# A table for PSUM tiles, an earlier ELU remainder and earlier cluster assignments in a fused attention and feed-forward kernel

## The chip, the cores and the metric

The kernel runs on one core of one Trainium2 chip. The metric is the device time of one execution in microseconds (us), as a median of several runs. The engines of the core are named as the profile names them: PE (TensorE, the matmuls; PEld its weight loads), DVE (VectorE), ACT (ScalarE), POOL (GpSimd) and SP (SyncE, which issues the DMAs here). Each engine works through its own queue of instructions in the order in which the program issues them, and waits for others by semaphores.

## The reference

```python
def _attn_ref(q, k, v, centroids):          # 4 batches, 8 heads, 768 tokens, 64 wide; 16 centroids a head
    q_assign = np.argmax(np.einsum('bhsd,hcd->bhsc', q_n, c_n), axis=-1)   # rows normalized
    k_assign = np.argmax(np.einsum('bhsd,hcd->bhsc', k_n, c_n), axis=-1)
    mask = q_assign[:, :, :, None] == k_assign[:, :, None, :]
    scores = np.where(mask, scale * np.matmul(q, k.transpose(0, 1, 3, 2)), -1000000000.0)
    attn = softmax(scores)
    return np.matmul(attn, v)

def _moe_ref(x, w_in, w_out):               # x: 3072 x 512, w_in: 512 x 2048, w_out: 2048 x 512
    h = x @ w_in
    g = np.where(h > 0.0, h, np.exp(np.minimum(h, 0.0)) - 1.0)
    return g @ w_out
```

The attention output, brought to 3072 tokens of 512, is the x of the second part. A query attends only to the keys that were assigned to the same centroid.

## The kernel before, in words

Work is cut into 48 blocks: 4 batches, each of 3 thirds of the queries (256 of them), each of 4 pairs of heads. One loop (lines 780 to 858) goes over the block number n and issues all instructions in an order that is written out by hand (the pool's scheduler is switched off in line 89). In one pass it issues, in this order: the values of the block before, `values(n - 1)`; what is left in a list, `finish()`; loads; the scores of block n, `scores(n)`; transposes for the next batch in passes 8 to 11 of a batch; and then two to four steps of the feed-forward part (`main`), which runs LAG = 7 blocks behind. `extra` hangs further steps behind single steps of `main`. So a pass is marked by what `main` holds, which repeats every four passes, `(n - 7) % 4`. The change calls it the kind:

- kind 0: two hidden products, `hidden` 0 and 1 (called h0 and h1 below)
- kind 1: two hidden products, `hidden` 2 and 3, and a `finish()` behind them
- kind 2: four of the seven products with w_out (`outer`, lines 651 to 717)
- kind 3: the other three

A batch has 12 blocks. Its last (n = 11, 23, 35) is of kind 0, the first of the next batch of kind 1.

The pieces that the steps below touch:

- `scores` (482 to 545): three units u0, u1, u2 of 128 x 2 x 512 each. A unit's matmuls (line 490) fill one pair of PSUM banks, ACT takes the exponential of it into p (line 513). In the first batch a further matmul per half adds a mask (line 502); in the others `keep_same` (442 to 456) zeroes on DVE, after the exponential, what belongs to other clusters, twelve instructions of line 449 per block. It needs kc and qc, the cluster numbers of keys and queries, which small matmuls (lines 417 and 430) and ACT copies (420 and 438) prepare.
- `sums` (547 to 551): three DVE additions that shrink the six parts of p for the row sums.
- `values` (553 to 598): o_bank takes p times v (line 572), a tile d takes the row sums (line 561). ACT reads d twice (590, 591), copies o_bank (592) and takes an exponential (593); DVE (594, 595) and POOL (598) finish the reciprocal and the scaling.
- `hidden` (606 to 626): 32 matmul instructions (line 613) into one pair tile, an exponential on ACT (623), a clamp on POOL (624). The remainder, `elu` (628 to 639), reads the pair tile once more on DVE (line 630) and then forms a difference (632 or 634). It isn't issued at once: `hidden` puts it into the list `lag`, and the next `finish()` issues it, which is that of the next `hidden`, or the one behind `values` in the next pass.
- `similar` (362 to 376): products of queries (j = 0) or keys (j = 1) with the centroids, for half of the tokens (line 369), and a DVE transpose out of PSUM (376). `assign` (378 to 405): reduce, compare, transpose on DVE (388, 392, 402), which gives the cluster rows `hot`. For the next batch both products are issued in the last pass of a batch, the assignment of the queries there too, that of the keys in the first pass of the next batch (lines 786 to 788).

PSUM has three pair tiles and two single banks, o_bank and f_bank. The pair tiles come from a pool with three buffers: every call of `banks()` gets a new tile, and the pool gives it a buffer that has been released by its last reader in the order of the program. In steady passes, with the buffers called A, B and C, this gives, as the program built from the kernel before has it:

| kind | d | u0, u1, u2 | hidden |
|---|---|---|---|
| 0 | C | B, A, C | B, A |
| 1 | C | B, C, B | A, C |
| 2 | B | A, C, B | |
| 3 | A | C, B, A | |

Of the kernel before, what the change touches and what calls it, by code (L numbers as in the profile page):

```python
# [9 lines left out]
F32 = mybir.dt.float32  # L10
# [7 lines left out]
PSUM = bass.MemoryType.PSUM  # L18

P = 128  # L20
# [41 lines left out]
def main_path(ctx, tc, c, q, k, v, centroids, moe_w_in, moe_w_out, out):  # L62
# [21 lines left out]
    probs = ctx.enter_context(tc.tile_pool(name="probs", bufs=NT // 2))  # L84
    work = ctx.enter_context(tc.tile_pool(name="work", bufs=2))
    xtp = ctx.enter_context(tc.tile_pool(name="xtp", bufs=2))
    short = ctx.enter_context(tc.tile_pool(name="short", bufs=3, space=PSUM))
    long = ctx.enter_context(tc.tile_pool(name="long", bufs=1, space=PSUM))
    ctx.enter_context(tc.manual_schedule())

# [1 line left out]
    o_bank = long.tile([P, 512], F32, name="o_bank")  # L92
    f_bank = long.tile([P, 512], F32, name="f_bank")

    def banks():
        return short.tile([P, 2, 512], F32, name="banks", tag="banks")


    g = const.tile([P, FC, QS], F32, name="gT")
# [259 lines left out]
                else:  # L359
                    nc.vector.tensor_copy(to[:, :, m], of)  # L360

    def similar(b, j, at, size):

        if at == 0:
            sim[b, j] = route.tile([P, S], F32, name="sim", tag="sim", bufs=1)
        ps = banks()[:, 0]
        cols = slice(at, at + size)
        for pr in range(NPR):
            nc.tensor.matmul(
                ps[32 * pr : 32 * pr + 32, :size],  # L370
                lhsT=cT[:, 32 * pr : 32 * pr + 32],
                rhs=T[b * NPR + pr, j][:, cols],
                start=True,
                stop=True,
            )
        return lambda: nc.vector.transpose(sim[b, j][:, cols], ps[:, :size])  # L376
# [34 lines left out]

    def key_numbers(b):

        ps = banks()[:, 0]
        kc[b] = route.tile([P, NT, H], F32, name="kc", tag="kc", bufs=2)
        for kt in range(NT):
            nc.tensor.matmul(
                ps[:, ts(kt, H)], lhsT=hot[b, 1][:, 0, ts(kt, P)], rhs=index, start=True, stop=True
            )
        nc.scalar.copy(kc[b].rearrange("p t h -> p (t h)"), ps[:, : NT * H])  # L420
# [21 lines left out]
    def keep_same(n):  # L442

        b, third, pr = blocks[n]
        for u in range(NT // 2):
            for e in range(2):
                for m in range(2):
                    p = pu[n, u][:, e, ts(m, QS)]
                    nc.vector.scalar_tensor_tensor(  # L449
                        p,  # L450
                        qc[b, third][:, 2 * pr + e],
                        kc[b][:, 2 * u + m, 2 * pr + e : 2 * pr + e + 1],
                        p,
                        op0=Alu.is_equal,
                        op1=Alu.mult,
                    )
# [18 lines left out]
    LAG = 7  # L475
# [2 lines left out]

    blocks = [(b, third, pr) for b in range(B) for third in range(NQ) for pr in range(NPR)]
    pu, osum, xT = {}, {}, {}  # L480

    def scores(n):
        b, third, pr = blocks[n]
        i = b * NPR + pr
        cols = ts(third, QS)

        def plain(s, kt):
            for e in range(2):
                rows = slice(64 * e, 64 * e + 64)
                nc.tensor.matmul(  # L490
                    s[:, e, ts(kt % 2, QS)],
                    lhsT=T[i, 1][rows, ts(kt, P)],
                    rhs=T[i, 0][rows, cols],
                    start=n > 0 or kt % 2 == 0,
                    stop=b > 0,
                    skip_group_check=n == 0,
                )

        def mask(s, kt):
            for e in range(2):  # L500
                rows = slice(64 * e, 64 * e + 64)
                nc.tensor.matmul(
                    s[:, e, ts(kt % 2, QS)],
                    lhsT=hot[b, 1][rows, side(pr, e), ts(kt, P)],
                    rhs=qm[n][rows],
                    start=False,
                    stop=True,
                    skip_group_check=n == 0,
                )

        def exponentials(s, u):
            p = pu[n, u] = probs.tile([P, 2, 2 * QS], F32, name="p", tag="p")
            nc.scalar.activation(p, s, Act.Exp, scale=SCALE)  # L513

        if n == 0:

            turn_first = similar(0, 1, 0, QS)
            turn_rest = similar(0, 1, QS, 2 * QS)
            units = [banks() for _ in range(2)]
            for u in range(2):  # L520
                for m in range(2):
                    plain(units[u], 2 * u + m)
            turn_first()
            for u in range(NT // 2):
                assign(0, 1, u * QS, QS)
                if u == 0:
                    turn_rest()
                if u == 1:
                    units.append(banks())
                    for m in range(2):  # L530
                        plain(units[2], 4 + m)
                for m in range(2):
                    mask(units[u], 2 * u + m)
                exponentials(units[u], u)
                weigh(1)
            return
        for u in range(NT // 2):
            s = banks()
            for m in range(2):
                plain(s, 2 * u + m)  # L540
                if b == 0:
                    mask(s, 2 * u + m)
            exponentials(s, u)
            if n < LAG + 3:
                weigh(1)
# [7 lines left out]
    def values(n):  # L553

        b, third, pr = blocks[n]
        d = banks()[:, 0]
        summed = osum.pop(n, None)

        def row_sums(p, m, kt, last):
# [46 lines left out]
        lag.clear()  # L606

    def hidden(b, third, n):
        h = banks()
        hf = h.rearrange("p a (f s) -> p (a f) s", f=2)  # L610
        for ch in range(KC):
            for f in range(4):
                nc.tensor.matmul(  # L613
                    hf[:, f],
                    lhsT=w_in[:, ch, ts(4 * n + f, P)],
                    rhs=xT[b, third][:, ch],
                    start=(ch == 0 and f % 2 == 0),
                    stop=(ch == KC - 1),
                    skip_group_check=True,
                )  # L620
        t = g[:, 4 * n : 4 * n + 4]

        nc.scalar.activation(t, hf, Act.Exp)  # L623
        nc.gpsimd.tensor_scalar(t, t, 1.0, 0.0, op0=Alu.min, op1=Alu.max)  # L624
        finish()
        lag.append(lambda: elu(n, t, hf))
# [103 lines left out]
    turns = {8: 0, 9: 1, 10: 2, 11: 3}  # L730
    groups = [g for b in range(B) for third in range(NQ) for g in mlp(b, third)]

    def clusters(b, j):
        for half in range(2):
            similar(b, j, half * HS, HS)()

    def load_v(n):
        b, third, pr = blocks[n]
# [21 lines left out]

    def verdict():
        ok = c["ok"]
        ps = banks()[:, 0]
        nc.tensor.matmul(ps[:1, :1], lhsT=ok[:, 3:4], rhs=ones[:, :1], start=True, stop=True)
        nc.vector.tensor_copy(c["go"], ps[:1, :1])

# [10 lines left out]
        assign(0, 0, half * HS, HS)  # L777
    masks(0)

    for n in range(len(blocks) + LAG):  # L780
        b, at = n // NB, n % NB
        ahead = b + 1 < B
        if n <= len(blocks) and n > 0:
            values(n - 1)
        finish()
        if at == 0 and 0 < b < B:
            for half in range(2):
                assign(b, 1, half * HS, HS)
        if ahead:
            for pr in {5: [0], 6: [1], 9: [2], 10: [3]}.get(at, []):  # L790
                load("q", (b + 1) * NPR + pr)
# [19 lines left out]
        if n < len(blocks):  # L811
            late = [lambda n=n: sums(n)] if n >= LAG + 3 else []
            if b > 0:
                third = at // NPR
                q_in = lambda b, third, places: (lambda: query_numbers(b, third, places))
                if at == 0:
                    extra[0] = [
                        lambda b=b: key_numbers(b),
                        q_in(b, third, [(0, f_bank), (1, o_bank)]),
                        lambda n=n: keep_same(n),  # L820
                    ] + late
                    extra[1] = [
                        lambda b=b, third=third: query_numbers(
                            b, third, [(2, f_bank), (3, banks()[:, 0])]
                        )
                    ]
                else:
                    if at % NPR == 0:
                        query_numbers(b, third, [(0, f_bank), (1, o_bank)])
                        extra[0] = [q_in(b, third, [(2, f_bank), (3, o_bank)])]  # L830
                    keep_same(n)
                    if len(main) == 3 and at % NPR == 2:
                        extra[1] = late
                    else:
                        late and late[0]()
            else:
                late and late[0]()
        if ahead and at + 1 == NB:

            extra[0] = [lambda b=b: clusters(b + 1, 0)]  # L840
            extra[1] = [
                lambda b=b: [assign(b + 1, 0, half * HS, HS) for half in range(2)],
                lambda b=b: clusters(b + 1, 1),
            ]
        for m, step in enumerate(main):
            step()
# [266 lines left out]
```

## Time and profile before

| what | us |
|---|---|
| median of 3 runs | 1018.0 (1017.7 to 1018.22) |
| the profiled execution, its own time | 1019.75 |
| its span, first to last instruction | 1017.6 |
| PE busy | 989.8 |
| DVE busy | 658.3 |
| ACT busy | 324.0 |
| POOL busy | 136.3 |
| mean granted PE clock | 0.994 of full speed |

The profile is one execution, recorded instruction by instruction. Its times are us from the start of the span. A row of the timeline has the start, the busy time, the engine, the line of the kernel, what is written from what and how many instructions were put together; in brackets stands how long the engine had been idle before and what ended that. A row of the waits has the waiting engine with its tile and line, what it waited for, and then the total, the number and the longest of these waits. Matmuls are pipelined and their ends are modelled, so that a busy PE isn't always a PE at its peak.

### The profile page before, as it was taken

How to read it: one execution, taken by the hardware profiler on the slowest of the kernel's cores; microseconds unless marked ns; L12 is line 12 of the kernel's file. 1: busy time of each engine (PE TensorE's matmuls, PEld its weight loads, DVE VectorE, ACT ScalarE, POOL GpSimd, SP SyncE). 2: the span in 40 equal slices, each digit the busy share in tenths (PEclk: the TensorE clock that was granted, in tenths of full speed). 3: DMA queues.
4: the chain of work that ended last, by engine and by line, in shares of the span. 5: the costliest groups of instructions: out<-in, count | busy, mean ns of one | idle time of the engine just before them, and what ended most of it. 6: DMA issues, size and time to landing. Idle time of an engine off the chain costs nothing.

```text
span 1017.6 us, 14770 instructions
## 1 busy us (share of the span) xinstructions
PE 989.8 (97%) x5989; PEld 773.3 (76%) x5989; DVE 658.3 (65%) x1182; ACT 324.0 (32%) x576; POOL 136.3 (13%) x145
## 2 busy tenths in 40 slices
PE   6999999999999999999999999999999999999997
PEld 4566777778878878777778778767887887888886
DVE  7999972576666667849567568577765665673121
ACT  6777422341242233222323232214223323321010
POOL 0010130110210210210111111111021021021010
PEclk9999999999999999999999999999999999999999
DMA  9857122000132122100122113101010010000000
GB/s 291 310 167 195 48 52 59 26 23 16 37 67 43 37 49 61 37 17 17 52 47 47 53 28 67 43 10 32 16 38 19 29 37 16 32 21 1 21 0 24
DMA packets 103963, 55.59 MB, mean 55 GB/s; under 512 B 83408, under 2 KB 96720, under 8 KB 103888
## 3 DMA queue, kind: packets, MB, share of 16 engines
q1 hardware_dynamic: 103888, 54.57, 19.3%
q8 instruction: 49, 0.80, 0.3%
q14 instruction: 26, 0.21, 0.1%
HBM read 48.27 MB, written 6.29 MB: 54 GB/s over the span
## 4 chain that ended last, share of the span: by engine, by line
PE 74%; DVE 17%; ACT 4%; issue 3%; DMA 1%; POOL 0%; DVEq 0%; ACTq 0%; POOLq 0%
PE banks L613 27%; PE f_bank L643 15%; PE o_bank L643 11%; PE o_bank L572 10%; PE banks L490 8%; DVE p L449 3%; DVE ex L265 2%; PE banks L561 2%; ACT p L513 1%; DVE w_in L268 1%; DVE w_out L268 1%; DVE w_in L271 1%; DVE ex L287 1%; DVE psum L550 1%; DVE w_out L271 1%
## 5 line engine op out<-in xcount | busy, mean ns | idle before, releaser
L613 PE MATMUL banks<-xT,w_in 128*128 128x256 f32 x1536 | 344.2, 384 | 4.3 <-DVE sim L376 3.9
L613 PEld LDWEIGHTS banks<-xT,w_in 128*128 128x128 f32 x1536 | 291.3, 191 | 54.1 <-DVE sim L376 6.1
L449 DVE SCALAR_TENSOR_TENSOR p<-qc,kc,p 128x256 f32<-128x256 uint8 x432 | 184.8, 500 | 18.2 <-ACT qc L438 18.1
L490 PE MATMUL banks<-qT,kT 64*128 64x256 f32 x1152 | 147.8, 389 | 5.6 <-ACT p L513 4.5
L572 PE MATMUL o_bank<-p,v_raw 128*64 128x256 f32 x1152 | 144.7, 386 | 2.4 <-DMA v_raw<-in_v_dram 1.6
L623 ACT ACTIVATE gT<-banks 128x1024 f32<-128x1024 f32 x48 | 49.1, 1024 | 293.4 <-PE banks L613 293.4
L513 ACT ACTIVATE p<-banks 128x1024 f32<-128x1024 f32 x144 | 140.2, 1033 | 4.0 <-PE banks L490 2.9
L490 PEld LDWEIGHTS banks<-qT,kT 64*128 64x128 f32 x1152 | 101.1, 186 | 45.1 <-PE o_bank L572 10.0
L572 PEld LDWEIGHTS o_bank<-p,v_raw 128*64 128x64 f32 x1152 | 78.2, 137 | 55.9 <-issue 14.5
L594 DVE TENSOR_TENSOR e<-e,r 128x256 f32<-128x256 f32 x48 | 20.4, 424 | 144.3 <-ACT r L593 144.3
L630 DVE SCALAR_TENSOR_TENSOR gT<-gT,banks 128x1024 f32<-128x1024 f32 x48 | 58.3, 1215 | 78.1 <-POOL gT L624 78.0
L624 POOL TENSOR_SCALAR gT<-gT 128x1024 f32<-128x1024 f32 x48 | 54.1, 1127 | 350.4 <-ACT gT L623 324.5
L590 ACT ACTIVATE r<-banks 128x256 f32<-128x256 f32 x48 | 18.4, 383 | 243.4 <-PE banks L561 243.4
L643 PE MATMUL o_bank<-w_out,gT 128*128 128x256 f32 x416 | 95.1, 382 | 0.0
L598 POOL TENSOR_TENSOR xT<-xT,r 128x256 f32<-128x256 f32 x48 | 40.2, 837 | 409.0 <-DVE r L595 354.4
L643 PEld LDWEIGHTS o_bank<-w_out,gT 128*128 128x128 f32 x416 | 78.2, 190 | 13.5 <-ACT p L513 2.0
L643 PE MATMUL f_bank<-w_out,gT 128*128 128x256 f32 x352 | 79.6, 379 | 0.0
L643 PEld LDWEIGHTS f_bank<-w_out,gT 128*128 128x128 f32 x352 | 66.9, 190 | 9.1
L643 PE MATMUL f_bank<-w_sum,gT 128*128 128x256 f32 x224 | 50.9, 380 | 0.5 <-DVE o_sb L683 0.2
L550 DVE TENSOR_TENSOR psum<-psum,p 128x1024 f32<-128x1024 f32 x38 | 50.2, 1322 | 1.4
L643 PEld LDWEIGHTS f_bank<-w_sum,gT 128*128 128x128 f32 x224 | 42.3, 190 | 7.4 <-DVE o_sb L683 1.7
L549 DVE TENSOR_TENSOR psum<-p 128x1024 f32<-128x1024 f32 x38 | 46.1, 1214 | 0.0
(130 smaller groups left out, 835.2 us busy)
## 6 DMA issues: line engine op xcount, KB each, us to landing
v_raw<-in_v_dram SPq DMA_DIRECT2D x48, 384.0 KB, 3.1
w_sum<-in_moe_w_out_dram SPq DMA_DIRECT2D x12, 512.0 KB, 5.3
out_dram<-o_sb SPq DMA_DIRECT2D x24, 256.0 KB, 2.0
q_raw<-in_q_dram SPq DMA_DIRECT2D x48, 96.0 KB, 3.3
k_raw<-in_k_dram SPq DMA_DIRECT2D x48, 96.0 KB, 2.9
w_sum<-in_moe_w_in_dram SPq DMA_DIRECT2D x8, 512.0 KB, 9.8
w_out<-in_moe_w_in_dram SPq DMA_DIRECT2D x8, 512.0 KB, 10.9
w_out<-in_moe_w_out_dram SPq DMA_DIRECT2D x4, 512.0 KB, 3.4
```

Source lines behind the costliest of these rows:

```text
L449: nc.vector.scalar_tensor_tensor(p, qc[b, third][:, 2 * pr + e], kc[b][:, 2 * u + m, 2 * pr + e : 2 * pr + e + 1], p, op0=Alu.is_equal, op ...
L490: nc.tensor.matmul(s[:, e, ts(kt % 2, QS)], lhsT=T[i, 1][rows, ts(kt, P)], rhs=T[i, 0][rows, cols], start=n > 0 or kt % 2 == 0, stop=b > 0 ...
L513: nc.scalar.activation(p, s, Act.Exp, scale=SCALE)
L549: nc.vector.tensor_tensor(to, pu[n, 0], pu[n, 1], op=Alu.add)
L550: nc.vector.tensor_tensor(to, to, pu[n, 2], op=Alu.add)
L572: nc.tensor.matmul(o_bank[64 * e : 64 * e + 64, :QS], lhsT=raw["v", n][:, e, kt], rhs=p[:, e, ts(m, QS)], start=(kt == 0), stop=(kt == NT ...
L598: nc.gpsimd.tensor_tensor(x, x, r, op=Alu.mult)
L613: nc.tensor.matmul(hf[:, f], lhsT=w_in[:, ch, ts(4 * n + f, P)], rhs=xT[b, third][:, ch], start=(ch == 0 and f % 2 == 0), stop=(ch == KC - 1),
L623: nc.scalar.activation(t, hf, Act.Exp)
L624: nc.gpsimd.tensor_scalar(t, t, 1.0, 0.0, op0=Alu.min, op1=Alu.max)
L630: nc.vector.scalar_tensor_tensor(t, t, -1.0, hf, op0=Alu.add, op1=Alu.max)
L643: nc.tensor.matmul(to[:, :QS], lhsT=left[:, f], rhs=right[:, f], start=(f == 0), stop=(f == FC // 2 - 1),)
```

## The change

The pool's three rotating buffers become three fixed pair tiles. `banks(i)` returns tile i modulo 3; without an argument (the start of the kernel) it takes turns. In the loop a table `place` says for each kind of block which tile d, the three units and the two hidden products use, counted from `at_tile`, which moves on by one in the passes of kinds 2 and 3 and in the first passes. In kind 1, u2 has the tile of h1; in kind 2, d and u1 share one.

For n > LAG, `finish()` is called in front of `values(n - 1)` too, so that a remainder left over from the pass before is issued ahead of the values.

In the last block of a batch both halves of one centroid product go to the two halves of one pair tile: the queries to u2's, the keys to h0's. The sums of that block move behind the query products, and the key assignment moves from the first pass of the next batch to the end of this one. In the first block of a batch the key numbers go to f_bank, and they, the numbers of the first head pair and `keep_same` are issued ahead of the hidden products; the numbers of the other pairs follow in two groups instead of one. At the very start the key products of block 0 go to o_bank and f_bank.

```diff
-    short = ctx.enter_context(tc.tile_pool(name="short", bufs=3, space=PSUM))
+    short = ctx.enter_context(tc.tile_pool(name="short", bufs=1, space=PSUM))
...
-    def banks():
-        return short.tile([P, 2, 512], F32, name="banks", tag="banks")
+    pair_tiles = [short.tile([P, 2, 512], F32, name=f"banks{n}") for n in range(3)]
+    turn_of = 0
+
+    def banks(i=None):
+        nonlocal turn_of
+        if i is None:
+            i = turn_of
+            turn_of = (turn_of + 1) % 3
+        return pair_tiles[i % 3]
...
-    def similar(b, j, at, size):
+    def similar(b, j, at, size, ps=None):
...
-        ps = banks()[:, 0]
+        if ps is None:
+            ps = banks()[:, 0]
...
     def key_numbers(b):
-        ps = banks()[:, 0]
+        ps = f_bank
...
-            turn_first = similar(0, 1, 0, QS)
-            turn_rest = similar(0, 1, QS, 2 * QS)
+            turn_first = similar(0, 1, 0, QS, o_bank)
+            turn_rest = similar(0, 1, QS, 2 * QS, f_bank)
...
         for u in range(NT // 2):
-            s = banks()
+            s = banks(place["u"][u])
...
-        d = banks()[:, 0]
+        d = banks(place["d"])[:, 0]
...
-        h = banks()
+        h = banks(place["h"][n % 2])
...
-    def clusters(b, j):
+    def clusters(b, j, i):
+        ps = banks(i)
+        for turn_half in [similar(b, j, half * HS, HS, ps[:, half]) for half in range(2)]:
+            turn_half()
+
+    def tell(b, j):
         for half in range(2):
-            similar(b, j, half * HS, HS)()
+            assign(b, j, half * HS, HS)
...
+    at_tile = turn_of
     for n in range(len(blocks) + LAG):
...
+        kind = (n - LAG) % 4 if n >= LAG else None
+        if kind == 1:
+            place.update(d=at_tile, u=[at_tile + 1, at_tile, at_tile + 2], h=[at_tile + 1, at_tile])
+        elif kind == 2:
+            place.update(d=at_tile + 2, u=[at_tile + 1, at_tile + 2, at_tile])
+        else:
+            place.update(d=at_tile, u=[at_tile + 1, at_tile + 2, at_tile])
+            place.update(h=[at_tile + 1, at_tile + 2])
+        if kind not in (0, 1):
+            at_tile += 1
+        if n > LAG:
+            finish()
         if n <= len(blocks) and n > 0:
             values(n - 1)
         finish()
-        if at == 0 and 0 < b < B:
-            for half in range(2):
-                assign(b, 1, half * HS, HS)
...
                 if at == 0:
-                    extra[0] = [
-                        lambda b=b: key_numbers(b),
-                        q_in(b, third, [(0, f_bank), (1, o_bank)]),
-                        lambda n=n: keep_same(n),
-                    ] + late
-                    extra[1] = [
-                        lambda b=b, third=third: query_numbers(
-                            b, third, [(2, f_bank), (3, banks()[:, 0])]
-                        )
-                    ]
-                else:
...
+                    key_numbers(b)
+                    query_numbers(b, third, [(0, o_bank)])
+                    extra[0] = [q_in(b, third, [(1, f_bank), (2, o_bank)])]
+                    extra[1] = [q_in(b, third, [(3, f_bank)])]
+                elif at % NPR == 0:
+                    query_numbers(b, third, [(0, f_bank), (1, o_bank)])
+                    extra[0] = [q_in(b, third, [(2, f_bank), (3, o_bank)])]
+                keep_same(n)
+            if b > 0 and at % NPR == 2:
+                extra[1] = late
+            elif not ahead or at + 1 < NB:
                 late and late[0]()
         if ahead and at + 1 == NB:
-            extra[0] = [lambda b=b: clusters(b + 1, 0)]
+            extra[0] = [lambda b=b, i=place["u"][2]: clusters(b + 1, 0, i)] + late
             extra[1] = [
-                lambda b=b: [assign(b + 1, 0, half * HS, HS) for half in range(2)],
-                lambda b=b: clusters(b + 1, 1),
+                lambda b=b: tell(b + 1, 0),
+                lambda b=b, i=place["h"][0]: clusters(b + 1, 1, i),
+                lambda b=b: tell(b + 1, 1),
             ]
```

## The prediction

> **What bounds the kernel.** I read the page's busy times first, then the waits of TensorE (PE), then the timeline around each wait, and last the stretches with the granted clock.
>
> ```profile
> PE 989.8 (97%) x5989; PEld 773.3 (76%) x5989; DVE 658.3 (65%) x1182; ACT 324.0 (32%) x576; POOL 136.3 (13%) x145
> ```
>
> PE is busy 989.8 of 1017.6 us, so the change can win only what PE loses. Of its waits (total us, times, longest) four fall on what the diff touches:
>
> ```profile
> PE banks L490 <- ACT p L513: 4.5, 10, 1.2
> PE banks L613 <- DVE sim L376: 3.9, 2, 2.0
> ...
> PE banks L490 <- DVE gT L630: 1.2, 3, 0.4
> ...
> PE banks L561 <- DVE psum L551: 0.5, 3, 0.2
> ```
>
> They understate the loss, since a matmul counts as busy until its modelled end (some 0.38 us, while the next starts 0.22 later). So I take the distance of starts in the timeline. Undisturbed, a block's 24 score matmuls take 2.79 us (start 261.05, next work 263.84), a hidden group of 32 takes 7.00 to 7.11, a pair of centroid products (x16) 1.43, a block's values 2.64 + 0.53.
>
> First place: kind 1, the block after a third's first two hidden groups.
>
> ```profile
> 281.02 2.11 PE L490 MATMUL banks<-qT,kT 64*128 64x256 f32 x16
> ...
> 282.40 1.95 ACT L513 ACTIVATE p<-banks 128x1024 f32<-128x1024 f32 x2
> ...
> 283.37 1.22 DVE L630 SCALAR_TENSOR_TENSOR gT<-gT,banks 128x1024 f32<-128x1024 f32 x1
> 283.49 1.14 PE L490 MATMUL banks<-qT,kT 64*128 64x256 f32 x8 [0.36 <-ACT p L513]
> ```
>
> The third unit stands still until the first unit's exponential is over (about 283.4): both got one pair tile, since h1, the hidden product just made, is still held by its remainder (L630), queued on DVE behind the values' L594/L595. Next work starts at 284.56: 3.54 us instead of 2.79. Natural start of the third unit: 282.93.
>
> Second place: the last block of a batch.
>
> ```profile
> 427.40 1.50 PE L369 MATMUL banks<-qT,cT 128*32 128x384 f32 x16
> ...
> 428.62 1.16 POOL L624 TENSOR_SCALAR gT<-gT 128x1024 f32<-128x1024 f32 x1 [7.74 <-ACT gT L623]
> 428.91 1.41 DVE L551 TENSOR_TENSOR psum<-psum 128x512 f32<-128x512 f32 x1
> 430.24 1.03 DVE L376 STREAM_TRANSPOSE sim<-banks 128x384 f32<-128x384 f32 x2
> 430.86 8.86 PE L613 MATMUL banks<-xT,w_in 128*128 128x256 f32 x32 [1.97 <-DVE sim L376]
> ```
>
> The second hidden group wants a tile that a transpose (L376) must empty, which stands behind the sums (L549 to L551). And the 8.86 us show a second price. Columns: busy us (count) of PE, PEld, DVE, ACT, POOL, then clock, DMA share, GB/s:
>
> ```profile
> 427.40:431.00 3.60, 1.63 (x18) 0.55 (x18) 3.53 (x5) 1.03 (x1) 1.16 (x1) 1.00 0.00 0
> 431.00:434.00 3.00, 3.00 (x10) 2.51 (x11) 2.93 (x5) 0.00 (x0) 0.00 (x0) 0.67 0.00 0
> ```
>
> After 1.97 us of idleness the granted clock fell to 0.67 in the next 3 us.
>
> **What the old order loses, by batch end.** At the second and third (427, 670): 2.04 (3.47 for the products instead of 1.43) + 1.78 (8.79 for the group instead of 7.01) + 0.83 (scores at 444.25: 3.62) + 0.99 after it (values at 462.86: 2.99 instead of 2.64, row sums 1.04 instead of 0.53, scores 2.92: DVE reached mask and sums late, since the key and query numbers came behind a hidden group) = 5.64. The first (188) has 0.16 + 0.83 + 0.99 = 1.98; there no masking on DVE delays the sums.
>
> **The change, part by part.**
> - *Table, kind 1.* u2 takes h1's tile, and finish() moves in front of the values, so L630 is queued ahead of L594. In the case shown the clamp (L624) of h1 ends at 280.10 and DVE is idle from 275.2 to 282.56: L630 runs 280.1 to 281.3, L632 to 282.0, both before u2's 282.93 and before L594's 282.56. The 0.75 goes, but for 0.05 (u1 waits for the reader of d as before). Six such blocks: 6 x 0.70 = 4.2. If the idle DVE stretch were gone, this would be 0. The seventh (115.3, first batch) waits 1.3; there L630 follows weight work that ends at 114.8, so it ends at 116.0 instead of letting PE go at 116.81: 0.75.
> - *Table, kind 2.* d now sits in u1's tile, not u2's. Kind 1 shows what that costs: u1 started 0.98 after u0 instead of 0.93. About nine blocks x 0.05 = -0.45 (bounds 0 and 1). Kinds 0, 3 and the start reuse tiles at the old distance: 0. The first batch's key products in o_bank and f_bank wait for nothing new; PE at 20 to 26 us waits for the cluster rows (L402, L405): 0, +-0.3.
> - *Batch end, PE.* Both query products lie in the two halves of u2's tile, free since 421.8; the second hidden group has u1's tile. It waits for no transpose: 2.04 and, with the gap, 1.78 go, twice, and 0.16 at the first. Key products go to h0's tile, which L630 of h0 must leave: from the list below 6.7 us after tau, wanted at 8.5. Key and query numbers come directly behind the scores, so masking starts at about 446.6 (scores' end 444.6 by the list below, 0.3 for the key numbers, 1.6 from L430 at 455.11 to L449 at 456.72) and not 456.7; with 5.1 for masks and 3.9 for sums it ends at 455.6, some 4 us before the values at about 460: 0.99 goes. Those 4 us are its cover; without them it stays. One more group of small matmuls (L430) adds a gap of 0.2 and 0.1 at the next hidden group (7.11 for 7.01): -0.3 each time, three times.
> - *Batch end, DVE: the new wait.* h1's remainder now stands behind sums, two pairs of transposes and two pairs of assignments, and u2 of the next block waits for it; behind u2 stand key numbers, query numbers and the next group on PE. With tau = end of the first hidden group (427.40): transposes from +0.95, free at 2.26; sums 1.26 + 1.26 + 0.72 (distances at 182.23) to 5.50; h0's remainder 1.82 (431.20 to 433.02) to 7.32; assignments 3.33 to 10.65; transposes 0.96 to 11.6; assignments 3.33 to 14.95; L630 1.2 to 16.15. PE: 1.43 + 7.10 + 1.43 + 3.17 + 1.91 = 15.04. So u2 waits 1.2, plus 0.15 of restart (the group after a stall took 1.07 instead of 0.93): 1.35. It takes the place of the 0.83, at all three ends, the first too, whose sums are now held behind transposes although DVE is idle there.
>
> Weighed here: SBUF — State Buffer, section "Who interferes with whom", says that a DVE instruction with two SBUF inputs and a GpSimd one that reads SBUF exclude each other for the whole instruction, whichever starts first. The trace has both cases: L551 took 1.41 beside L624 and 0.69 alone. In my list the last L392 of the first assignments starts at 9.55, and the clamp of h1 at 9.75 (group end 8.53, and 1.22 from there as from 427.40 to 428.62), so DVE is first and POOL waits, which hurts nobody. Were DVE 0.2 later, L392 would wait until 10.8 and the stall be 2.4. I take 1.35, the order of the sum, and keep 1.0 and 2.4.
>
> Sum: 4.2 + 0.75 - 0.45 + first end (1.98 - 1.35 - 0.3 = 0.33) + two ends of 5.64 - 1.65 = 3.99 each (7.98) = 12.8 us. The profiled execution took 1019.75 us (span 1017.6 and 2.15 around it), so 1007.0 for such a one; it lies 1.75 above the median 1018.0, so the forecast is 1018.0 - 12.8 = 1005.2.
>
> **Rivals.**
> 1. *The stall at batch ends is long and cools the clock.* Stall 2.4 instead of 1.35 (three times: 3.15) leaves PE idle about 2.0 us. TensorE: Matmul & The Clock Gate, section "HAM oscillation — how this bites in real kernels", puts the limit at gaps over about 3.4 us; by it nothing more is lost and the time is 1008.4. The row speaks against the rule: 1.97 us sufficed here (while 1.57 at 36.7, before a value load, did not), and cost 1.78. By the row three falls add 5.3: 1013.7. For it: the 0.2 us of margin. Against: needs DVE later than each row says. 0.12.
> 2. *The table helps only at batch ends.* If L630 in front of the values isn't done by 282.9, u2 waits for it instead of the exponential. For it: in the old trace DVE did run L630 at 283.37. Against: it only stood behind L594, and DVE was idle. Gain without 4.95: 1010.1. 0.05.
> 3. *Slower: the remainder behind the assignments takes more than all that is won.* At each batch end DVE's list would be X longer than summed. 12.8 - 3X - 5.3 falls below -2 at X = 3.2 us, as if one pair of assignments (3.33) were counted too few; at X = 4 the time is 1022.5. For it: DVE's list is the longest in the kernel. Against: each of its entries is a measured row. 0.03; between X = 1.9 and 3.2 there is no change that can be told: 0.03.
>
> **How the numbers follow.** The summed case has 0.77; its own ends are 1003.5 (stall 1.0, kind 2 free, some 0.3 at the start) and 1009 (stall 2.4 without a fall, kind 2 at 1). The range 1002.5 to 1010.5 takes in rival 2 and leaves out the clock falls and rival 3. A measurement of this kernel can tell about 0.2%, 2 us, from no change. Faster 0.94, same 0.03, slower 0.03.
>
> **What would show it.** Right: no gap at L613 from L376, no clock below 1.0 near batch ends, L630 before L594 in kind 1, scores 2.84 there, and as PE's one wait for DVE L630 three gaps of about 1 us at L490. Wrong: gaps at L490 from L630 in kind 1 (rival 2), or a clock of 0.67 after batch ends (rival 1), or a wait that shows at L417 or L430, which I put at nothing.

## The result and the profile after

The changed kernel takes 1010.25 us (median of 4, 1009.18 to 1012.78) beside 1018.11 for the kernel before: a ratio of 0.9923, with a 95% interval of 0.9899 to 0.9947. Measured a second time it took 1010.47 (7 executions, 1008.98 to 1016.18; 0.9912, 0.9893 to 0.9931). So it gains 7.9 us where 12.8 were forecast. The profiled execution took 1012.78 us (span 1010.8) and is the longest of the four. Line numbers have shifted by 7 to 9: scores are L499 now, the hidden product L622, the remainder L639, the compare of an assignment L400, the clamp L633 (one to three more in the kernels with an added delay).

The page and the waits of PE after the change:

```profile
PE 989.1 (98%) x5989; PEld 773.8 (77%) x5989; DVE 657.1 (65%) x1182; ACT 323.1 (32%) x576; POOL 136.0 (13%) x145
```

```profile
PE banks L499 <- DVE gT L639: 4.5, 4, 2.0
PE o_bank L581 <- ACT p L522: 2.1, 7, 0.8
```

PE works as long as before. The waits for the first unit's exponential and for the transpose are gone; in their place stand four waits for the remainder, the longest of 2.0 us (three such waits before, none over 0.4). Kind 1 within a batch now looks like this (timeline):

```profile
283.35 1.22 DVE L639 SCALAR_TENSOR_TENSOR gT<-gT,banks 128x1024 f32<-128x1024 f32 x1 [4.95 <-POOL gT L633]
283.71 0.60 PE L570 MATMUL banks<-psum,ones 128*64 128x256 f32 x4
...
284.24 2.98 PE L499 MATMUL banks<-qT,kT 64*128 64x256 f32 x24
...
285.77 0.42 DVE L603 TENSOR_TENSOR e<-e,r 128x256 f32<-128x256 f32 x1 [0.48 <-ACT r L602]
...
287.15 0.28 PE L438 MATMUL f_bank<-hot,index 32*128 32x256 bf16 x1
```

The remainder (L639) has ended at 284.57, before the values' DVE steps (L603) and before u2, the third of the units that are put together in the row of L499. The scores take 2.91 us (284.24 to 287.15, the start of the next work) instead of 3.54.

The next table shows where the time went, between the same starts of values (L572 and L581) in both traces. Its last column sorts the terms of the prediction's sum into these stretches; the 0.16 of the first batch's transposes lies ahead of the values of block 11.

| stretch | before | after | difference | forecast |
|---|---|---|---|---|
| start to the values of block 11 | 198.62 | 197.61 | -1.01 | -0.86 |
| first batch end, to the values of block 13 | 42.73 | 46.96 | **+4.23** | -0.12 |
| second batch within | 172.98 | 171.83 | -1.15 | -1.30 |
| second batch end | 69.49 | 65.90 | -3.59 | -3.94 |
| third batch within | 172.97 | 171.83 | -1.14 | -1.30 |
| third batch end | 69.49 | 65.90 | -3.59 | -3.94 |
| fourth batch, to PE's last start | 285.72 | 284.69 | -1.02 | -1.30 |

All stretches but one come within 0.4 us of the forecast. The first batch end lost 4.2. Here is the timeline of the changed kernel there and at the second end (a compare of the query assignment, the clamp and the remainder of h1, the third unit's matmuls):

```profile
197.39 1.04 POOL L633 TENSOR_SCALAR gT<-gT 128x1024 f32<-128x1024 f32 x1 [7.49 <-ACT gT L632]
197.43 1.42 DVE L400 SCALAR_TENSOR_TENSOR oh<-sim,top 128x384 bf16<-128x384 f32 x1
...
203.61 1.18 DVE L639 SCALAR_TENSOR_TENSOR gT<-gT,banks 128x1024 f32<-128x1024 f32 x1
...
204.85 2.08 PE L499 MATMUL banks<-qT,kT 64*128 64x256 f32 x8 [1.97 <-DVE gT L639]
...
207.65 9.16 PE L622 MATMUL banks<-xT,w_in 128*128 128x256 f32 x32
...
439.17 0.56 DVE L400 SCALAR_TENSOR_TENSOR oh<-sim,top 128x384 bf16<-128x384 f32 x1
439.22 1.42 POOL L633 TENSOR_SCALAR gT<-gT 128x1024 f32<-128x1024 f32 x1 [7.49 <-ACT gT L632]
...
444.50 1.18 DVE L639 SCALAR_TENSOR_TENSOR gT<-gT,banks 128x1024 f32<-128x1024 f32 x1
...
445.73 1.13 PE L499 MATMUL banks<-qT,kT 64*128 64x256 f32 x8 [1.03 <-DVE gT L639]
```

At the first end the clamp on POOL began 40 ns ahead of the compare on DVE, and the compare took 1.42 us instead of 0.56: it was held up while the clamp ran. At the second end the compare was ahead by 50 ns, and the clamp took 1.42 instead of 1.04, for which nobody waits. So PE waits 1.03 us for the remainder at the second end and 1.97 at the first. And behind the longer wait the clock was halved (stretches of the changed kernel; the columns are those of the prediction):

```profile
200.00:204.90 4.90, 2.94 (x26) 1.72 (x22) 4.73 (x11) 3.15 (x7) 0.00 (x0) 1.00 0.28 80
204.90:211.70 6.80, 6.80 (x26) 4.74 (x27) 4.48 (x12) 1.60 (x3) 0.72 (x1) 0.50 0.00 0
```

The next hidden group took 9.09 us (207.65 to 216.74) instead of 7.10. From the values of the batch's last block to the next values it is 26.87 us at the first end (197.61 to 224.48) and 22.78 at the second (439.43 to 462.21): the longer wait and the slow clock cost 4.1.

### The profile page after: what moved, and what is told of

Same layout as the page of the kernel before. It is cut to its first block, busy times and chain, and to the rows that moved or that the text cites. A ratio compares the mean times of both kernels' runs of the same rounds, so it can differ in the third digit from the quotient of the medians.

```text
span 1010.8 us, 14691 instructions
## 1 busy us (share of the span) xinstructions
PE 989.1 (98%) x5989; PEld 773.8 (77%) x5989; DVE 657.1 (65%) x1182; ACT 323.1 (32%) x576; POOL 136.0 (13%) x145
## 4 chain that ended last, share of the span: by engine, by line
PE 81%; DVE 15%; issue 1%; ACT 1%; DMA 0%; POOL 0%; SPq 0%; DVEq 0%; POOLq 0%; ACTq 0%
PE banks L622 29%; PE f_bank L652 16%; PE o_bank L652 12%; PE banks L499 10%; PE o_bank L581 10%; PE banks L570 2%; DVE ex L272 2%; DVE w_in L275 1%; DVE gT L639 1%; DVE w_in L278 1%; DVE w_out L275 1%; DVE ex L294 1%; DVE oh L400 1%; DVE w_out L278 1%; DVE hot L410 1%
## 5 line engine op out<-in xcount | busy, mean ns | idle before, releaser
L622 PE MATMUL banks<-xT,w_in 128*128 128x256 f32 x1536 | 342.8, 383 | 0.3 <-POOL xT L607 0.3
L622 PEld LDWEIGHTS banks<-xT,w_in 128*128 128x128 f32 x1536 | 290.4, 191 | 49.0 <-issue 9.9
L499 PE MATMUL banks<-qT,kT 64*128 64x256 f32 x1152 | 147.7, 391 | 4.5 <-DVE gT L639 4.5
L581 PE MATMUL o_bank<-p,v_raw 128*64 128x256 f32 x1152 | 144.6, 386 | 2.1 <-ACT p L522 2.1
L639 DVE SCALAR_TENSOR_TENSOR gT<-gT,banks 128x1024 f32<-128x1024 f32 x48 | 58.4, 1216 | 131.5 <-POOL gT L633 131.5
L499 PEld LDWEIGHTS banks<-qT,kT 64*128 64x128 f32 x1152 | 101.6, 187 | 42.9 <-issue 17.8
L581 PEld LDWEIGHTS o_bank<-p,v_raw 128*64 128x64 f32 x1152 | 78.2, 137 | 55.8 <-issue 14.8
L633 POOL TENSOR_SCALAR gT<-gT 128x1024 f32<-128x1024 f32 x48 | 53.2, 1109 | 336.2 <-ACT gT L632 330.4
L603 DVE TENSOR_TENSOR e<-e,r 128x256 f32<-128x256 f32 x48 | 20.4, 425 | 86.6 <-ACT r L602 86.6
```

What stands on the lines that cost most here:

```text
L499: nc.tensor.matmul(s[:, e, ts(kt % 2, QS)], lhsT=T[i, 1][rows, ts(kt, P)], rhs=T[i, 0][rows, cols], start=n > 0 or kt % 2 == 0, stop=b > 0 ...
L581: nc.tensor.matmul(o_bank[64 * e : 64 * e + 64, :QS], lhsT=raw["v", n][:, e, kt], rhs=p[:, e, ts(m, QS)], start=(kt == 0), stop=(kt == NT ...
L622: nc.tensor.matmul(hf[:, f], lhsT=w_in[:, ch, ts(4 * n + f, P)], rhs=xT[b, third][:, ch], start=(ch == 0 and f % 2 == 0), stop=(ch == KC - 1),
L639: nc.vector.scalar_tensor_tensor(t, t, -1.0, hf, op0=Alu.add, op1=Alu.max)
```

## The experiments

The theory to be tested has three parts. At each batch end DVE's list, from the first hidden group to h1's remainder, is 1.2 us longer than what PE has to do meanwhile. At the first end the mutual exclusion of compare and clamp adds 0.9. And a gap of 1.97 us on PE may halve the clock. The rivals are: the spread and the loss have other causes; the sums had to go behind the transposes; the new table isn't what brings the wait. Each kernel ran beside the kernel before, the first four with 1017.95 us for it, the next four with 1017.83, then two with 1017.94. The ratios in brackets are the recorded ones with their 95% intervals; they are not the quotients of two medians, and can differ from these by 0.002.

**The changed kernel again.** 

> The changed kernel once more, unaltered, for comparison on the same chip. My theory: u2 of the first block of a batch waits for the remainder of h1 at all three batch ends, 1.4 us at two of them and 2.3 at the first, where the compare of an assignment (0.56 us) began 40 ns after the clamp on POOL and stood until that was over (1.42). The long wait leaves PE idle for 1.97 us, and the clock may fall after it, by how the wait lies to the 3.41 us steps in which the clock changes: 1009.2 without the fall, 1011.3 to 1012.8 with it. Rival: the spread has nothing to do with the first batch end; then the execution with a clock of 0.998 has the same gaps there as that with 0.995.

Measured: 1010.47. Four executions with a mean clock of 0.998 took 1008.98 to 1010.47, three with 0.992 took 1012.34 to 1016.18. In the traced one, of 1016.18, the clamp was 30 ns ahead at the first end (201.11 and 201.14), the gap was 1.97 us, and the clock fell at 208.75. Its time also holds a gap of 3.04 us at 36.5 with a clock fall at 38.09. Of the untraced executions only the mean clock is known, so this run alone doesn't tell whether the short ones had the gap without the fall; the last experiment shows that for another kernel.

**Sums in front.**

```diff
-            elif not ahead or at + 1 < NB:
+            else:
                 late and late[0]()
...
-            extra[0] = [lambda b=b, i=place["u"][2]: clusters(b + 1, 0, i)] + late
+            extra[0] = [lambda b=b, i=place["u"][2]: clusters(b + 1, 0, i)]
```

> The changed kernel with one part undone: the sums of a batch's last block stand in front of the query transposes again. Theory (the wait is the length of DVE's list behind the first hidden group): the sums fill DVE's idle time of 2 us and more ahead of the transposes, the list ends about 1.2 us earlier at two ends and 2.2 at the first, u2 waits 0.1 to 0.3, no clock fall behind a batch end: 1005.0 to 1006.0. Rival (the sums had to go behind, since the second hidden group waits for the transposes): a gap of some 2 us comes back in front of the second hidden group at two ends, and the time is 1012 or more.

Measured: 1006.36 (0.9879; 0.9859 to 0.9898), 0.4 above the expected range. No gap came back in front of the second hidden group, so the rival is out. By the traces it gains 4.77 us at the first end and 0.66 at each of the others, not the 1.2 expected. Its timeline at the second end shows why:

```profile
434.73 2.81 PE L581 MATMUL o_bank<-p,v_raw 128*64 128x256 f32 x24
434.87 1.05 DVE L384 STREAM_TRANSPOSE sim<-banks 128x384 f32<-128x384 f32 x2 [1.06 <-PE banks L377]
...
439.13 1.18 DVE L639 SCALAR_TENSOR_TENSOR gT<-gT,banks 128x1024 f32<-128x1024 f32 x1
...
440.37 1.13 PE L499 MATMUL banks<-qT,kT 64*128 64x256 f32 x8 [0.37 <-DVE gT L639]
```

DVE now runs out of work for 1.06 us and waits for PE's key products. What follows these on DVE (transposes, assignments, remainder: 434.87 to 440.31) is by itself 0.5 longer than what PE has to do meanwhile, the values and two units. No clock fall was recorded behind any batch end.

**A later clamp.** A small copy on ACT whose result nobody uses delays the clamp (`nudge` is a tile of its own):

```diff
+        if n == 1 and ahead and at + 1 == NB:
+            nc.scalar.copy(nudge, hf[:, 0, :32])
         nc.scalar.activation(t, hf, Act.Exp)
```

> The changed kernel with an ACT copy of 32 columns (about 0.2 us) ahead of the exponential of h1 in each batch's last block, so that the clamp on POOL starts some 0.2 us later; its result is not used. Theory (whichever of the clamp and the compare starts first holds the other up): at the first end the compare now starts first and takes 0.56, u2 waits 1.4 as at the other ends, no clock fall: 1008.0 to 1008.6, with little spread. Rival (the first end is late for another reason, or a later clamp only makes the remainder later): first end as in the changed kernel, 1009 to 1013.

Measured: 1008.51 (0.9896; 0.9877 to 0.9915), all five within 1008.31 to 1008.70. At the first end the compare is 50 ns ahead now and takes 0.56 us (timeline):

```profile
197.92 0.56 DVE L401 SCALAR_TENSOR_TENSOR oh<-sim,top 128x384 bf16<-128x384 f32 x1
197.97 1.41 POOL L636 TENSOR_SCALAR gT<-gT 128x1024 f32<-128x1024 f32 x1 [7.58 <-ACT gT L635]
...
204.49 1.13 PE L500 MATMUL banks<-qT,kT 64*128 64x256 f32 x8 [1.11 <-DVE gT L642]
```

Additional work on ACT has made the kernel 2 us faster (from 1010.47), and steady.

**A later assignment.** The opposite delay: `for _ in range(3): nc.vector.memset(nudge, 0.0)` at the start of `tell(b, 0)`, so that the compare comes later.

> The changed kernel with three small memsets on DVE (about 0.1 us each, unused) ahead of the query assignments of the next batch. Theory: at the second and third end the compare now starts after the clamp, stands until it is over (1.3 to 1.4 instead of 0.56), and u2's wait grows from 1.4 to 2.3 or 2.5 there too, with clock falls at more ends (1.7 to 3.2 us each): 1011 to 1018. Rival (no exclusion): only the memsets themselves are added, at most 0.3 at each end: 1009.9 to 1013.7.

Measured: 1013.52, twelve executions from 1010.87 to 1019.56: five with a mean clock of 0.987 to 0.989 took 1019.05 to 1019.56, six with 0.996 or 0.997 took 1010.87 to 1012.27. The median lies in the range of the theory and, just, in that of the rival (1009.9 to 1013.7), so it is the trace that decides. In it the compares at all three ends start behind the clamp and take 1.09, 1.16 and 1.16 us instead of 0.56, PE waits 1.97 us at all three, and the clock fell behind each. At the second end (timeline):

```profile
437.80 1.04 POOL L634 TENSOR_SCALAR gT<-gT 128x1024 f32<-128x1024 f32 x1 [7.49 <-ACT gT L633]
438.09 1.16 DVE L401 SCALAR_TENSOR_TENSOR oh<-sim,top 128x384 bf16<-128x384 f32 x1
```

Two opposite delays of 0.2 to 0.3 us turn the order round in opposite ways, and it is each time the second of the two instructions that takes longer: the exclusion is shown.

**The table without the early remainder** (the two lines `if n > LAG: finish()` taken out).

> The changed kernel with the call of the remainder in front of the values taken out; the table stays. Theory (the table alone would be a loss, since u2 then waits for a remainder that stands behind the values' two DVE steps): in kind 1 u2 starts at the end of L639, some 1.8 us later than it would, instead of the 0.7 that the kernel before loses there: seven times 1.8 over the changed kernel, and 0.9 more at each batch end with more clock falls: 1022 to 1032, slower than the kernel before. Rival, as in my prediction's second case (the table then helps only at batch ends and is else neutral): about 1014.

Measured: 1030.23, slower than before (1.0106; 1.0079 to 1.0134). Its waits for the remainder, and one block of kind 1 in its timeline:

```profile
PE banks L499 <- DVE gT L639: 16.7, 10, 2.8
```

```profile
287.07 0.43 DVE L604 SCALAR_TENSOR_TENSOR r<-e,r 128x256 f32<-128x256 f32 x1
287.42 0.08 DVE L604 DVE_READ_ACCUMULATOR r<-e,r 128x1 f32 x1
287.42 1.22 DVE L639 SCALAR_TENSOR_TENSOR gT<-gT,banks 128x1024 f32<-128x1024 f32 x1
288.67 0.69 DVE L641 TENSOR_TENSOR gT<-gT 128x512 f32<-128x512 f32 x1
288.69 1.13 PE L499 MATMUL banks<-qT,kT 64*128 64x256 f32 x8 [1.51 <-DVE gT L639]
```

The remainder (L639) stands behind the values' steps (L604), and u2 waits for it: 1.77 us more than in the changed kernel in each of the six blocks of kind 1 within the later batches. So the two parts of the change are one: u2's new tile without the earlier remainder costs more than the old wait.

**Old tile for u2.** In kind 1, `u=[at_tile + 1, at_tile, at_tile + 1], h=[at_tile + 2, at_tile]`.

> The changed kernel with the first line of the table put back: in kind 1 u2 shares u0's tile and the hidden product takes h1's. Theory: u2 waits for u0's exponential again, 0.63 more in six blocks and 0.8 in the first batch, but at the batch ends this wait is shorter than that for the remainder (0.83 instead of 1.4, 1.4 and 2.3) and too short for a clock fall: +4.6 - 2.6 against the changed kernel without its clock falls, so 1010.5 to 1011.5 with little spread. Rival (the wait at batch ends is not u2's tile): the batch ends keep their 1.4 to 2.3 and the time is 1013 to 1017.

Measured: 1016.22, above the expected range, for a reason beside the question. In the last third no scores stand between h1 and the next hidden product, which now took h1's tile and waited 3.5 us for the remainder; with a clock fall that is 5.8 us in the trace.

```profile
PE banks L622 <- DVE gT L639: 3.8, 2, 3.5
```

Within the later batches the scores of each block of kind 1 take 0.63 more (3.54 instead of 2.91), as expected. With the old choice of tiles in the passes without scores:

> The variant with u2 back on u0's tile in kind 1, this time with the old choice of tiles for the hidden products behind the last block, where no scores are: my first version of it made a hidden product of the last third wait 3.5 us for the remainder of h1, with a clock fall after it, 5.8 us in all by its trace. Theory: 1016.2 less 5.8, that is 1010.0 to 1010.8, little spread: the new table is worth 4.6 within the batches, but its wait at the batch ends takes 2.6 of that, and clock falls more. Rival (u2's tile is worth its whole 4.6): 1013 to 1014.

Measured: 1010.64 (0.9926; 0.9912 to 0.9939), as the theory had it. The batch ends lose their wait for the remainder, so it is u2's new tile that brings it.

**Only the batch ends.** The kernel of the last experiment without the early remainder.

> The same without the call of the remainder in front of the values, so that of the whole change only the new order of the batch ends (and fixed tiles) is left. Theory (the early remainder has its worth only through u2's tile, as nobody else waits for it): no change against the variant above, within 0.5: 1009.6 to 1011.0. Rival (the early remainder is worth something by itself, since the values' DVE steps or the masks come sooner): 1 us or more apart.

Measured: 1011.37 (0.9931; 0.9917 to 0.9944), 0.7 apart, between the two expectations. The two traces differ by 1.6 before block 2, where the executions' start differs, and by 0.79 at the first batch end, where the next hidden product waits 0.72 for the remainder; else they agree. So the expectation that nobody else waits for the remainder failed at one place. Of the 7.5 us that the change gains by these medians, 6.6 come from the batch ends and 0.7 from the early remainder. The new tile of u2 adds nothing that can be told (1010.64 to 1010.47, well within the spread of the changed kernel): what it wins within the batches is spent at their ends.

**A better order.** First the sums in front and the key assignment back in the first pass of the next batch, behind the remainder:

```diff
         if n > LAG:
             finish()
+        if at == 0 and 0 < b < B:
+            tell(b, 1)
...
-                lambda b=b: tell(b + 1, 1),
```

> Sums of a batch's last block in front again, and the key assignment put back to the first pass of the next batch, between the remainder and the values. Theory: DVE now reaches h1's remainder as soon as the key products are transposed, so u2 waits for nothing, and the key numbers wait 0.1 to 0.3 us for the assignment: 0.4 to 0.6 less at each of three ends than with the sums alone in front (1006.4): 1004.6 to 1005.3. Rival (the wait moves to the key numbers in full): 1006.4.

Measured: 1005.32 (0.9871; 0.9853 to 0.9890), at the upper end of the expected range; each end takes 0.38 less in the traces. Then, with two more entries of the table (kind 2: `u=[at_tile + 1, at_tile, at_tile + 2]`; kind 1 within later batches: u1 and u2 exchanged):

> The same as the one with sums in front and the key assignment behind the remainder, and two more entries of the table changed: in kind 2 u1 takes h3's tile and u2 that of d, and in kind 1 within a batch (not in the first) u1 takes h1's and u2 that of d. Theory (u1 loses 0.12 by waiting for d's readers, 0.05 in my prediction): 0.12 x (10 + 6) less, 1003.0 to 1003.6. Rival (the wait for d's readers is hidden or moves to u2): no change against that kernel.

Measured: 1003.88 (0.9857; 0.9838 to 0.9875), the fastest of all, though 0.3 above the expected range. Each of the 13 places at which the traces differ gives 0.11 or 0.12, 1.5 in all and not 1.9, since three of the sixteen blocks that I counted don't gain.

**The clock.** Two further single executions of the kernel with late assignments: 

> The kernel with late assignments once more, for its gaps of about 1.97 us at three batch ends and the clock behind each. Theory (the clock is decided in fixed steps of 3.41 us, and falls where the gap lies in one step): an execution near 1011 has the same three gaps, each split over two steps with no more than about 1.4 us in either, and no fall; one near 1019.5 has them whole. Rival (the fall follows from the gap's length alone): 1.97 us is followed by a fall every time, and an execution without falls has shorter gaps.

> The same once more: each execution lies differently to the steps. Theory: falls behind whole gaps, none behind split ones. Rival: falls behind every gap of 1.97 us.

Measured: 1011.04 and 1020.47, both with three gaps of 1.96 or 1.97 us, the first without a fall at the batch ends, the second with three. The clock changes in steps: the recorded falls of a trace start whole multiples of 3.413 us apart (25.86, 432.04 and 674.39 before the change are 119 and 71 of them). The 0.67 that the prediction read behind 431 us is the mean over a full clock until 432.04 and half of it from there. Here are the stretches around the first gap (202.75 and 202.76), cut at these steps, in the first execution and then in the second:

```profile
200.54:203.95 3.41, 2.21 (x18) 1.38 (x16) 3.27 (x9) 3.14 (x7) 0.00 (x0) 1.00 0.42 115
203.95:207.37 3.42, 2.66 (x21) 1.95 (x22) 2.16 (x5) 1.49 (x4) 0.72 (x1) 1.00 0.00 0
```

```profile
201.26:204.67 3.41, 1.50 (x14) 0.82 (x10) 3.31 (x8) 2.72 (x6) 0.00 (x0) 1.00 0.40 115
204.67:208.09 3.42, 3.36 (x17) 2.05 (x18) 1.46 (x5) 1.24 (x3) 0.72 (x1) 0.50 0.00 0
```

The same gap, split 1.21 and 0.75 over two steps, left the clock alone; with 1.91 in one step, it halved it. So the theory holds, with one number off: a split of 1.76 and 0.20 (third end of the first execution) was let pass too, so the "1.4" of the expectation was too small. All kept traces together say the same. Between the first 30 us and the end of the kernel, each of the 17 steps in which PE stood idle for 1.81 us or more was followed by a half clock, and none of those with 1.39 or less. Between 1.49 and 1.76 it went both ways: in the kernel without the early remainder, whole gaps of 1.5 us were followed by a fall twice (287 and 857) and once not (612). The Trainium skill, page TensorE: Matmul & The Clock Gate, section "What's actually happening", states such a free-running step of 3413 ns, and the traces agree; that it takes a whole idle step of about 3.4 us, as the same section has it, is not what they show.

## Why the prediction was right, and where not

The direction, the mechanism and the order of size were right. The median lies in the range, 0.25 us below its upper end, and that is in part luck: the range left out clock falls, which came in some of the executions, and its upper part was there for rival 2, which did not come; five of the eleven executions lie above it. The likeliest case (1005.2) was 5 us too fast.

- *Table and early remainder within the batches:* right. The gain is 0.63 instead of 0.70 each, because u1's wait for the readers of d is 0.12, not 0.05: that small term was mis-sized by reading a start distance in the old trace. Kind 2 shows the same 0.12 in four of its ten blocks. The block of kind 1 in the first batch gave 0.81 (0.75).
- *Batch ends, PE:* right. No wait for a transpose, no clock fall behind it; the key and query numbers ahead of the hidden product brought 0.87 (0.99).
- *Batch ends, the new wait:* named and sized rightly at two ends. The scores there took 4.20 us instead of 2.79, a loss of 1.41 (1.35). A slip lies in its sum: the list's own ends, 16.15 and 15.04, are 1.11 apart, where the text takes 1.2; u2 started 1.22 late.
- *The step that failed:* "the last L392 of the first assignments starts at 9.55, and the clamp of h1 at 9.75 [...], so DVE is first". The clamp came at 9.74 (197.39 less 187.65), the compare at 9.78 at the first end and 9.70 at the second. The term behind it is "transposes from +0.95", which is read from the first batch end before the change. Before and after (timelines; the products, then the transposes):

```profile
188.50 1.50 PE L369 MATMUL banks<-qT,cT 128*32 128x384 f32 x16
189.45 1.20 DVE L376 STREAM_TRANSPOSE sim<-banks 128x384 f32<-128x384 f32 x2 [3.98 <-PE banks L369]
```

```profile
187.65 1.50 PE L377 MATMUL banks<-qT,cT 128*32 128x384 f32 x16
189.28 1.05 DVE L384 STREAM_TRANSPOSE sim<-banks 128x384 f32<-128x384 f32 x2 [7.83 <-PE banks L377]
```

Both halves' products are now issued ahead of the first transpose, and this began when all of them had ended, at 1.63 and 1.57 (189.28 and 431.04). So the sums began 0.3 us later than in the list, the compare about 0.2, and of the margin of 0.2 us nothing was left. "I take 1.35, the order of the sum" became true of two ends and false of one: there it was 2.3 with a clock fall behind it, and the stretch had +4.23 instead of -0.12. The longer wait and the fall, 4.1 us, are most of the 5.5 us by which the gain between the traces, 7.27, falls short of 12.8; the rest are the terms above and small differences at the other ends.
- *The last step of the sum* was off too, by up to 1.75. It took the 12.8 from the median, 1018.0, though this gain was read from an execution of 1019.75 and holds its two clock falls of 1.78; for such a one the prediction itself has 1007.0. The executions of the kernel before lie in steps of about that size: near 1016 with mean clocks of 0.997 and 0.998, near 1017.8 mostly with 0.995 and 0.996, those above 1019 with 0.992 to 0.995. So the median one probably had one fall less to lose. That is worked out from mean clocks; no trace of it was kept.
- *Rival 1* came true in its mechanism at one end of three, and in part of the executions; it was priced for all three only (1013.7, 0.12). The likeliest case should have been a mixture, with one end lost in some executions.
- *Rival 2* was priced too low. It was put at 1010.1, neutral within the batches. The case nearest to it, the table with the remainder behind the values, is 12 us slower than the kernel before, its longer batch ends and clock falls among them.
- *Weighed against pages:* the exclusion in the Trainium skill, SBUF — State Buffer, section "Who interferes with whom", holds here in both directions (the compare took 1.42 or the clamp 1.42, whichever was second). Against the 3.4 us of TensorE: Matmul & The Clock Gate, section "HAM oscillation — how this bites in real kernels", the prediction's own row was right: 1.97 us sufficed.
- That the sums moved behind the transposes would cost something at the first end was in the forecast; that it is the costliest line of the change (4.1 us by medians) was not. It wasn't needed: with the query products in one tile, the second hidden group no longer waits for a transpose.

Open: which of the untraced executions had a fall at which place, why a fall lasts one step or two, and what beside the idle time in a step decides between 1.5 and 1.8 us.

## What to carry to other kernels

A buffer given to a new user brings that user behind everything that its last reader is queued behind. So list the reader's engine from the last common point, beside what the waiting engine does meanwhile, and put long work into the list's idle times. Where two entries of such a sum lie within its error, price both orders, each as a case of its own. When a change has removed a wait, look again at what had been moved out of the way for it. And take a gain that was read from one execution from the time of that execution.

## What was not expected of the hardware

- 40 ns in the start of two instructions on DVE and POOL decided over 0.9 us of PE's wait, and, together with the clock fall behind it, over 4.1 us of the whole; 0.2 us of added ACT work made the kernel 2 us faster and narrowed five executions to 0.4 us.
- A gap of 1.97 us on PE halved the clock in one execution and not in another of the same kernel, by where it lay to steps of 3.41 us; with three such gaps, one kernel's executions spread from 1010.9 to 1019.6 us.
